# Shared PSUM slots, 4 KB loads and strided transposes in a fused recurrence and highway layer

**Chip and metric.** One core of one Trainium2 chip. The time is device microseconds (us) of one execution; every time quoted is a median over runs, every ratio a comparison on the same chip in the same rounds.

## The reference

The input is 4 sequences of 6,336 tokens with 256 channels (25,344 tokens, 26 MB in fp32). A gated recurrence runs over each sequence, and a highway layer follows:

```python
sig = 1 / (1 + exp(-f_logit))
f = lower_bound + (1 - lower_bound) * sig
for t in range(S):
    h = f[:, t] * h + (1 - f[:, t]) * x[:, t];  y[:, t] = h
H = maximum(y @ w_h, 0);  T = 1 / (1 + exp(-(y @ w_t + b_t)))
out = T * H + (1 - T) * y
```

## The kernel before

The work goes in units of 1,024 tokens (24, and one last of 768). Tokens are loaded with tokens on the partitions, but this program's scans take channels there (128x1024 in their records), so TensorE transposes in and back. One unit takes these steps; each has a letter, and the string PLAN gives the order in which they are issued, engine by engine.

- L, X: load `f_logit` and `x`. U: ScalarE makes u = sigmoid(-f_logit). P: GpSimd makes bv = u*x, two tokens at a time, interleaved so that a pair of bf16 values is one 4-byte word.
- A, B: TensorE transposes u and the pairs of bv into PSUM, the memory in which this program puts TensorE's results (`uT`, `bT`). F: ScalarE turns uT into the decay f. S: VectorE scans y = f*y + b.
- Z, G: products of y with w_t and w_h (`zp`, `gp`). T: ScalarE's sigmoid t. D: VectorE's d = max(-y, gp). E and H: e = d*t, columns shared between VectorE and GpSimd.
- O: y and e transposed back and added in PSUM (`op`), four tokens per partition a group. C and V: copies of op on ScalarE (and VectorE, for the last pieces). R: store.

In code (cuts marked; each PSUM product has a tile of its own name, hence one buffer):

```python
    BUFS = dict(lt=5, xt=5, o=8, u=4, bv=2, f=6, t=2, d=2, e=2, y=7)
    pools = {k: ctx.enter_context(tc.tile_pool(name=k + "pool", bufs=n)) for k, n in BUFS.items()}
    singles = ctx.enter_context(tc.tile_pool(name="singles", bufs=1))
    ps1 = ctx.enter_context(tc.tile_pool(name="ps1", bufs=1, space=bass.MemoryType.PSUM))

    def pairs(t):
        return t.rearrange("p (k j) d -> p k (j d)", j=2)

    def tokens(src, u, j0, j1, j):
        np_, _, b, per, a = units[u]
        if per == NB:
            return src[b, a + j0 * np_:a + j1 * np_, :].rearrange("(k p j) d -> p k (j d)", p=np_, j=j)
        return src[b + j0 // per:b + j1 // per, a:a + per * np_, :].rearrange("b (p j) d -> p b (j d)", j=per)

    def load(i, name, src):
        u, j0, j1 = fronts[i]
        np_ = units[u][0]
        t = fs[i][name] = new(name, [NB, D], FP32)
        pin(nc.sync.dma_start(pairs(t[:np_, :j1 - j0]), tokens(src, u, j0, j1, 2)))

    def gpsimd_mul(out_, a, b):
        ins = pin(nc.gpsimd.tensor_mul(out_, a, b))
        # ... cut: orders it behind the parts of e that VectorE was given before it (the list `port`) ...

    def product(i, k):
        np_, _ = shape(fronts[i])
        if k == 0:
            fs[i]["bv"] = new("bv", [NB // 2, D, 2], BF16)
        gpsimd_mul(inner(fs[i]["bv"][:np_, k:k + 1])[:, 0], fs[i]["u"][:np_, 2 * k:2 * k + 2],
                   fs[i]["xt"][:np_, 2 * k:2 * k + 2])

    def psum(piece, m, s, key, dtype):
        t = ps1.tile([P, NB * P], dtype, tag=key, name=key)
        for c, h in enumerate(halves(piece)[m]):
            s[key, h] = t[:, c * 512:c * 512 + width(piece)]
            yield s[key, h], h

    def decay_act(i, h):
        np_, N = shape(fronts[i])[0], width(fronts[i])
        f = fs[i]["f", h] = new("f", [NB * P], FP16)
        pin(nc.scalar.activation(f[:, :N].rearrange("p (k q j) -> p k q j", q=np_, j=2),
                                 fs[i]["uT", h].rearrange("p (k j q) -> p k q j", q=np_, j=2), AF.Identity,
                                 scale=ncc[:, h:h + 1], bias=1.0))

    def b_pe(i, m):
        np_, nb = shape(fronts[i])
        for bT, h in psum(fronts[i], m, fs[i], "bT", BF16):
            for k in range(nb // 2):
                pin(nc.tensor.transpose(bT[:, 2 * k * np_:2 * (k + 1) * np_].bitcast(FP32),
                                        fs[i]["bv"][:np_, k, h * P:(h + 1) * P].rearrange("p d j -> p (d j)").bitcast(FP32),
                                        ident_f[:np_, :np_]))

    # ... scan: h = f*h + b along the columns, on VectorE; ffn_pe: products with w_t and w_h; t_act, d_dve: ScalarE and VectorE ...

    SHARE = 448          # columns of e that GpSimd takes, of 1024

    def e_dve(j):
        port.append(pin(nc.vector.tensor_mul(*e_cols(j, 0, width(backs[j]) - shared(j)))))

    def e_pool(j):
        gpsimd_mul(*e_cols(j, width(backs[j]) - shared(j), width(backs[j])))

    def o_pe(j, q):
        op = bs[j]["op", q] = ps1.tile([P, QB, D], FP32, tag="op", name="op")
        (np_, nb), y = shape(backs[j]), y_of(j)
        j0, j1 = q * QB, min((q + 1) * QB, nb)
        g = min(j1 - j0, units[backs[j][0]][3])
        for k in range(j0, j1):
            b, i = divmod(k - j0, g)
            cols = slice((j0 + b * g) * np_ + i, (j0 + (b + 1) * g) * np_, g)
            for h in range(NH):
                o = op[:np_, k - j0, h * P:(h + 1) * P]
                pin(nc.tensor.matmul(o, y[:, h, cols], diag[:, h], start=True, stop=False))
                pin(nc.tensor.matmul(o, bs[j]["e"][:, h, cols], ident_b, start=False, stop=True))

    def o_copy(j, q, engine):
        np_ = shape(backs[j])[0]
        if ("o", q) not in bs[j]:
            bs[j]["o", q] = new("o", [QB, D], FP32)
        g, a = copied(j, q)
        part = slice(0, a) if engine is nc.scalar else slice(a, g)
        copy = nc.scalar.copy if engine is nc.scalar else nc.vector.tensor_copy
        pin(copy(bs[j]["o", q][:np_, part], bs[j]["op", q][:np_, part]))

    # ... kinds: one letter for each step ...
    PLAN = (
        # ... seven lines cut ...
        "OGFCTAOESDPHPPUCBZGOSDFTCBAZGORRRXRRRRXPHPUFTCSDEBAGZOSDFFTCABZGOFTCPPHRRRSSDEZGOBTFCRDGOZHSDDESCROT"
        "TCEVRGZOTTCDDVROEVCROCVR"
    )
    for k in PLAN:
        kinds[k][0](*next(todo[k]))
```

Of the kernel before, what the change touches and what calls it, by code (L numbers as in the profile page):

```python
# [19 lines left out]
def kernel(  # L20
# [43 lines left out]

    HELPED = 3



    first = ctx.enter_context(tc.tile_pool(name="first", bufs=1))
# [14 lines left out]
    def pin(ins):  # L84
        return tc.keep_in_program_order(ins)

    def pairs(t):

        return t.rearrange("p (k j) d -> p k (j d)", j=2)

    def inner(t):

        return t.rearrange("p k d j -> p k j d")
# [1 line left out]
# [6 lines that stand above are left out]

    def load(i, name, src):
        u, j0, j1 = fronts[i]
        np_ = units[u][0]
        t = fs[i][name] = new(name, [NB, D], FP32)
        pin(nc.sync.dma_start(pairs(t[:np_, :j1 - j0]), tokens(src, u, j0, j1, 2)))

    def shape(piece):

# [43 lines left out]
    def gpsimd_mul(out_, a, b):  # L153

        ins = pin(nc.gpsimd.tensor_mul(out_, a, b))  # L155
        while port:
            tc.add_manual_dep(ins.ins, port.pop().ins.name, mybir.DependencyInfo(
                mybir.DependencyClass.Sync, mybir.DependencyReason.DATA), reason="shared port")

    def product(i, k):  # L160
        np_, _ = shape(fronts[i])
        if k == 0:
            fs[i]["bv"] = new("bv", [NB // 2, D, 2], BF16)
        gpsimd_mul(inner(fs[i]["bv"][:np_, k:k + 1])[:, 0], fs[i]["u"][:np_, 2 * k:2 * k + 2],
                   fs[i]["xt"][:np_, 2 * k:2 * k + 2])

    def width(piece):
        np_, nb = shape(piece)
# [3 lines left out]

        return ((0,), (1,)) if width(piece) > 512 else ((0, 1),)

    def psum(piece, m, s, key, dtype):

        t = ps1.tile([P, NB * P], dtype, tag=key, name=key)
        for c, h in enumerate(halves(piece)[m]):
            s[key, h] = t[:, c * 512:c * 512 + width(piece)]
            yield s[key, h], h  # L180

    def decay_pe(i, m):
        np_, nb = shape(fronts[i])
        for uT, h in psum(fronts[i], m, fs[i], "uT", FP16):
            for j in range(nb):
                pin(nc.tensor.transpose(uT[:, j * np_:(j + 1) * np_], fs[i]["u"][:np_, j, h * P:(h + 1) * P],  # L186
                                        ident_h[:np_, :np_]))

    def decay_act(i, h):

        np_, N = shape(fronts[i])[0], width(fronts[i])
        f = fs[i]["f", h] = new("f", [NB * P], FP16)
        pin(nc.scalar.activation(f[:, :N].rearrange("p (k q j) -> p k q j", q=np_, j=2),  # L193
                                 fs[i]["uT", h].rearrange("p (k j q) -> p k q j", q=np_, j=2), AF.Identity,
                                 scale=ncc[:, h:h + 1], bias=1.0))

    def b_pe(i, m):
        np_, nb = shape(fronts[i])
        for bT, h in psum(fronts[i], m, fs[i], "bT", BF16):

            for k in range(nb // 2):
                pin(nc.tensor.transpose(bT[:, 2 * k * np_:2 * (k + 1) * np_].bitcast(FP32),  # L202
                                        fs[i]["bv"][:np_, k, h * P:(h + 1) * P].rearrange("p d j -> p (d j)").bitcast(FP32),
                                        ident_f[:np_, :np_]))

# [17 lines left out]
        u, j0, j1 = backs[j]  # L223
        return ys[u][:, :, j0 * units[u][0]:j1 * units[u][0]]

    def ffn_pe(j, m, key, k):
        N = width(backs[j])
        for p, h in psum(backs[j], m, bs[j], key, FP32):
            for ki in range(NH):
                for a in range(0, N, 512):  # L230
                    e = min(a + 512, N)
                    pin(nc.tensor.matmul(p[:, a:e], w_sb[:, k, ki, h * P:(h + 1) * P], y_of(j)[:, ki, a:e],  # L232
                                         start=ki == 0, stop=ki == NH - 1))
# [9 lines left out]
        pin(nc.vector.scalar_tensor_tensor(bs[j]["d"][:, m, :width(backs[j])], y_of(j)[:, m], ncc[:, m:m + 1],  # L243
                                           bs[j]["gp", m], op0=ALU.mult, op1=ALU.max))

    SHARE = 448

    def shared(j):

# [5 lines left out]
        return (bs[j][key][:, :, a:e] for key in "edt")  # L255

    def e_dve(j):
        port.append(pin(nc.vector.tensor_mul(*e_cols(j, 0, width(backs[j]) - shared(j)))))  # L258

    def e_pool(j):  # L260
        gpsimd_mul(*e_cols(j, width(backs[j]) - shared(j), width(backs[j])))

    QB = NB // 2

    def o_pe(j, q):

        op = bs[j]["op", q] = ps1.tile([P, QB, D], FP32, tag="op", name="op")
        (np_, nb), y = shape(backs[j]), y_of(j)
        j0, j1 = q * QB, min((q + 1) * QB, nb)
        g = min(j1 - j0, units[backs[j][0]][3])  # L270
        for k in range(j0, j1):
            b, i = divmod(k - j0, g)
            cols = slice((j0 + b * g) * np_ + i, (j0 + (b + 1) * g) * np_, g)
            for h in range(NH):
                o = op[:np_, k - j0, h * P:(h + 1) * P]
                pin(nc.tensor.matmul(o, y[:, h, cols], diag[:, h], start=True, stop=False))  # L276
                pin(nc.tensor.matmul(o, bs[j]["e"][:, h, cols], ident_b, start=False, stop=True))  # L277

    def copied(j, q):

        g = min(QB, shape(backs[j])[1] - q * QB)
        return g, g // 2 if j >= len(backs) - HELPED else g

    def o_copy(j, q, engine):
        np_ = shape(backs[j])[0]
        if ("o", q) not in bs[j]:
            bs[j]["o", q] = new("o", [QB, D], FP32)
        g, a = copied(j, q)
        part = slice(0, a) if engine is nc.scalar else slice(a, g)
        copy = nc.scalar.copy if engine is nc.scalar else nc.vector.tensor_copy  # L290
        pin(copy(bs[j]["o", q][:np_, part], bs[j]["op", q][:np_, part]))  # L291

    def store(j, q):
        u, j0, _ = backs[j]
        a, (g, _) = j0 + q * QB, copied(j, q)
        per = min(g, units[u][3])
        pin(nc.sync.dma_start(tokens(out_bsd, u, a, a + g, per),
                              bs[j]["o", q][:units[u][0], :g].rearrange("p (k j) d -> p k (j d)", j=per)))

    def each(pieces, count):  # L300
        return [(i, k) for i, piece in enumerate(pieces) for k in range(count(piece))]

    def groups(piece):
        return -(-shape(piece)[1] // QB)


    kinds = {
# [1 line left out]
        "X": (lambda i, _: load(i, "xt", x), each(fronts, lambda p: 1)),  # L309
        "Q": (lambda i, k: load_weights(k), [(0, 0), (0, 1)]),  # L310
        "U": (lambda i, _: gate(i), each(fronts, lambda p: 1)),
        "P": (product, each(fronts, lambda p: shape(p)[1] // 2)),
        "A": (decay_pe, each(fronts, lambda p: len(halves(p)))),
        "F": (decay_act, each(fronts, lambda p: NH)),
        "B": (b_pe, each(fronts, lambda p: len(halves(p)))),
        "S": (scan, each(fronts, lambda p: NH)),
        "W": (lambda i, h: weights(h), [(0, 0), (0, 1)]),
        "Z": (lambda j, m: ffn_pe(j, m, "zp", 1), each(backs, lambda p: len(halves(p)))),
        "T": (t_act, each(backs, lambda p: NH)),
        "G": (lambda j, m: ffn_pe(j, m, "gp", 0), each(backs, lambda p: len(halves(p)))),  # L320
        "D": (d_dve, each(backs, lambda p: NH)),
        "E": (lambda j, _: e_dve(j), each(backs, lambda p: 1)),
        "H": (lambda j, _: e_pool(j), [(j, 0) for j in range(len(backs)) if shared(j)]),
        "O": (o_pe, each(backs, groups)),
        "C": (lambda j, q: o_copy(j, q, nc.scalar), each(backs, groups)),
        "V": (lambda j, q: o_copy(j, q, nc.vector), [p for p in each(backs, groups) if p[0] >= len(backs) - HELPED]),
        "R": (store, each(backs, groups)),
    }

    PLAN = (  # L330
        "XLLXLXQQLXUUAPFFBAPSSUFFBASSWLLXLXPFFUPBAPFFUUPWSSLLXXLXPPGABZPPFFTDSSGABZUFFTDSSEAGBZFUFUTHPPPPPPDS"
        "SOGABZCFTDSSAOGHPPPPFABZDSUFCTGBZALLXLXXLLRUTUFDSBGEESDOZBAGCTUFSDPPPPHZOBASTCFGZOBAPPPPHTCFDSZGOABD"
        "ESTUCFGZOABTFCDZAGOHPPPPFTCSDEEAGBOZXXRRLRRRRLLXFUCTDSAGBOZDSPHPPPFCTAOBZGESDFCOBATUFPPPPHPPZGATFCSD"
        "BZGAOTFCUSDPPHBZGAOXRRXXLRXLRRRTFCSDEBGAZOFTCESDABZGOPPPPPPHFTUCSDABGZOSEDPPHFTCABZGOFTUCSDRRXLLXRRR"
        "XBZGAOSDTFCBAGOZPHPPPPSDEFUTCBAGZOSDFTCABZGOPPHPPSDEFTCXLLRRRRBGAOZESDUFCTBOAGZSPHPPPPPPUFTCBADSGZOB"
        "FTCDESAGOZBHPPPPUCFTDSOGAZBCTFDSOGZBAHPCTUFDEESGZOABXRRRXRLLXLLRRDSTFCPPPPPHZGAOBTFCDSZGOBAUTCDSPPPH"
        "ZGODEFTCUBZAGOFTCESDABZGOFTCUSDPPHPPHPPPABZGOSDRXRRLRRRLXTCFBZOAGSEDTCFBZAGOTUCFSDBZGOAPPPPPHTCSDEZB"
        "OGFCTAOESDPHPPUCBZGOSDFTCBAZGORRRXRRRRXPHPUFTCSDEBAGZOSDFFTCABZGOFTCPPHRRRSSDEZGOBTFCRDGOZHSDDESCROT"
        "TCEVRGZOTTCDDVROEVCROCVR"
    )  # L340
    assert all(PLAN.count(k) == len(places) for k, (_, places) in kinds.items())
    todo = {k: iter(places) for k, (_, places) in kinds.items()}
    for k in PLAN:
        kinds[k][0](*next(todo[k]))
# [1 line left out]
_INS = ['x', 'f_logit', 'lower_bound', 'moe_w_h', 'moe_w_t', 'moe_b_t']  # L346
_OUTS = [((25344, 256), 'float32')]
# [25 lines left out]
```

## Time and profile before

| | before |
|---|---|
| time | 219.93 us (3 runs, 219.38 to 220.0) |
| span of the profiled run | 219.6 us |
| VectorE / ScalarE / TensorE / GpSimd busy | 90 / 89 / 86 / 73% |
| DMA packets in the main queue | 34,176, taking 92.1% of 16 engines |

The span is what the profiler sees of one execution, about 2 us under its time. The engine lines, slices, windows, head and tail are shown in the prediction below.

### The profile page before, as it was taken

Reading aid. Unit: us, or ns where it says so; the run is one execution under the profiler, and the core shown is the slowest. Engines: PE = TensorE matmul, PEld = TensorE weight load, DVE = VectorE, ACT = ScalarE, POOL = GpSimd, SP = SyncE. Lnnn points to the kernel's source line nnn. Section 1 sums busy time; section 2 is a strip of 40 time slices with the busy share of each in tenths; the row PEclk is TensorE's granted clock in tenths of the full one; section 3 lists DMA queues with packets and bytes.
Section 4 is the critical chain, followed back from the end, with each engine's and each line's share of the span. In section 5 each row is a group of like instructions: output and inputs, shape, how many; then the busy total and the mean of one; then the engine's idle time right before and its main releaser. Section 6 shows DMA issues by size and latency. Waiting matters only on the chain.

```text
span 219.6 us, 4569 instructions
## 1 busy us (share of the span) xinstructions
PE 188.4 (86%) x1772; PEld 132.9 (61%) x1800; DVE 197.2 (90%) x154; ACT 195.4 (89%) x194; POOL 161.1 (73%) x136
## 2 busy tenths in 40 slices
PE   0578787799999999999998999999999969998840
PEld 0435554466776766776766677566767656766640
DVE  1488978999999999999999999999999997999931
ACT  3679999999999999999999999999999958987621
POOL 4758579699769697889986979599687769663200
PEclk9999999999999999999999999999999997999975
DMA  5999999999999999999999999999999992644553
GB/s 146 401 408 408 411 403 408 409 404 409 405 416 415 403 414 404 411 417 409 409 410 407 402 418 416 409 408 406 416 413 413 349 357 112 215 169 168 212 213 103
DMA packets 34741, 78.68 MB, mean 358 GB/s; under 512 B 2336, under 2 KB 2848, under 8 KB 34720
## 3 DMA queue, kind: packets, MB, share of 16 engines
q1 hardware_dynamic: 34176, 78.39, 92.1%
q8 instruction: 14, 0.23, 0.4%
q10 hardware_dynamic: 544, 0.00, 0.1%
q14 instruction: 7, 0.06, 0.1%
HBM read 52.43 MB, written 25.95 MB: 357 GB/s over the span
## 4 chain that ended last, share of the span: by engine, by line
PE 29%; DVE 25%; DMA 15%; ACT 14%; issue 9%; POOL 4%; SPq 1%; DVEq 0%; POOLq 0%; ACTq 0%
DVE y L217 13%; PE gp L232 9%; DMA xt<-in_x_dram 9%; DVE d L243 8%; PE zp L232 6%; DMA lt<-in_f_logit_dram 5%; ACT t L238 5%; ACT f L193 4%; ACT o L291 4%; PE bT L202 4%; PE op L276 4%; PE op L277 3%; PE uT L186 3%; POOL bv L155 3%; DVE e L258 2%
## 5 line engine op out<-in xcount | busy, mean ns | idle before, releaser
L155 POOL TENSOR_TENSOR bv<-u,xt 128x512 bf16<-128x512 f16 (+1 forms) x100 | 114.3, 1173 | 30.8 <-DVE e L258 8.7
L217 DVE TENSOR_TENSOR_SCAN y<-f,y,bT 128x1024 bf16<-128x1024 f16 (+3 forms) x56 | 106.7, 1919 | 2.1 <-PE bT L202 2.0
L243 DVE SCALAR_TENSOR_TENSOR d<-y,ncc,gp 128x1024 bf16<-128x1024 bf16 (+1 forms) x52 | 62.7, 1209 | 3.0 <-PE gp L232 2.9
L193 ACT ACTIVATE f<-uT,ncc 128x1024 f16<-128x1024 f16 (+3 forms) x60 | 59.7, 1007 | 2.3 <-PE uT L186 2.3
L291 ACT COPY o<-op 128x1024 f32<-128x1024 f32 (+2 forms) x50 | 51.1, 1021 | 10.8 <-PE op L277 8.1
L238 ACT ACTIVATE t<-zp,bt 128x1024 bf16<-128x1024 f32 (+1 forms) x52 | 58.0, 1120 | 1.9 <-PE zp L232 1.0
L232 PEld LDWEIGHTS <-w_sb 128*128 128x128 f16 x400 | 38.2, 99 | 35.3 <-issue 4.4
L276 PE MATMUL op<-diag,y 128*128 128x128 f16 (+1 forms) x400 | 51.6, 222 | 3.5 <-ACT o L291 1.8
L155 POOL TENSOR_TENSOR e<-d,t 128x896 bf16<-128x896 bf16 x24 | 45.9, 1911 | 11.8 <-DVE e L258 5.0
L232 PE MATMUL gp<-y,w_sb 128*128 128x512 bf16 (+1 forms) x189 | 51.8, 387 | 2.9 <-DVE d L243 1.5
L277 PE MATMUL op<-ident_b,e 128*128 128x128 bf16 (+1 forms) x400 | 51.6, 222 | 2.5 <-POOL e L155 2.2
L149 ACT ACTIVATE u<-lt 128x2048 f16<-128x2048 f32 (+3 forms) x30 | 49.6, 1657 | 3.3 <-DMA lt<-in_f_logit_dram 3.1
L277 PEld LDWEIGHTS <-e 128*128 128x128 bf16 (+1 forms) x400 | 45.5, 116 | 10.6 <-issue 3.3
L232 PE MATMUL zp<-y,w_sb 128*128 128x512 bf16 (+1 forms) x183 | 49.5, 377 | 0.9
L276 PEld LDWEIGHTS <-y 128*128 128x128 bf16 (+1 forms) x400 | 45.7, 116 | 3.9
L186 PE MATMUL uT<-ident_h,u 128*128 128x128 f16 (+1 forms) x400 | 32.5, 227 | 8.6 <-ACT u L149 6.8
L202 PE MATMUL bT<-ident_f,bv 128*128 128x128 f32 (+1 forms) x200 | 32.4, 284 | 7.5 <-DVE y L217 5.9
L186 PEld LDWEIGHTS <-u 128*128 128x128 f16 (+1 forms) x400 | 27.5, 102 | 16.6 <-ACT u L149 8.2
L202 PEld LDWEIGHTS bT<-ident_f,bv 128*128 128x128 f32 (+1 forms) x200 | 22.0, 144 | 14.9 <-issue 5.5
L258 DVE TENSOR_TENSOR e<-d,t 128x1152 bf16<-128x1152 bf16 (+1 forms) x26 | 20.7, 817 | 0.5 <-ACT t L238 0.5
L217 DVE TENSOR_TENSOR_SCAN y<-f,bT 128x512 bf16<-128x512 f16 (+2 forms) x8 | 10.5, 1341 | 3.6 <-PE bT L202 3.6
L291 DVE COPY o<-op 128x512 f32<-128x512 f32 (+1 forms) x4 | 2.8, 690 | 4.8 <-DMA out_dram<-o 3.2
(19 smaller groups left out, 7.5 us busy)
## 6 DMA issues: line engine op xcount, KB each, us to landing
out_dram<-o SPq DMA_DIRECT2D x48, 512.0 KB, 11.4
lt<-in_f_logit_dram SPq DMA_DIRECT2D x21, 1024.0 KB, 13.9
xt<-in_x_dram SPq DMA_DIRECT2D x21, 1024.0 KB, 13.9
lt<-in_f_logit_dram SPq DMA_DIRECT2D x5, 512.0 KB, 8.0
xt<-in_x_dram SPq DMA_DIRECT2D x5, 512.0 KB, 9.1
lt<-in_f_logit_dram SPq DMA_DIRECT2D x2, 384.0 KB, 11.4
xt<-in_x_dram SPq DMA_DIRECT2D x2, 384.0 KB, 5.4
out_dram<-o SPq DMA_DIRECT2D x2, 384.0 KB, 3.0
```

The costliest lines, as they stand in the source:

```text
L149: pin(nc.scalar.activation(u[:np_, :nb], fs[i]["lt"][:np_, :nb], AF.Sigmoid, scale=-1.0))
L155: ins = pin(nc.gpsimd.tensor_mul(out_, a, b))
L186: pin(nc.tensor.transpose(uT[:, j * np_:(j + 1) * np_], fs[i]["u"][:np_, j, h * P:(h + 1) * P], ident_h[:np_, :np_]))
L193: pin(nc.scalar.activation(f[:, :N].rearrange("p (k q j) -> p k q j", q=np_, j=2), fs[i]["uT", h].rearrange("p (k j q) -> p k q j", q=np_, ...
L202: pin(nc.tensor.transpose(bT[:, 2 * k * np_:2 * (k + 1) * np_].bitcast(FP32), fs[i]["bv"][:np_, k, h * P:(h + 1) * P].rearrange("p d j -> ...
L217: pin(nc.vector.tensor_tensor_scan(y, fs[i]["f", h][:, c:c + w], fs[i]["bT", h][:, c:c + w], 0.0 if prev is None else prev, op0=ALU.mult, ...
L232: pin(nc.tensor.matmul(p[:, a:e], w_sb[:, k, ki, h * P:(h + 1) * P], y_of(j)[:, ki, a:e], start=ki == 0, stop=ki == NH - 1))
L238: pin(nc.scalar.activation(bs[j]["t"][:, m, :width(backs[j])], bs[j]["zp", m], AF.Sigmoid, bias=bt[:, m:m + 1]))
L243: pin(nc.vector.scalar_tensor_tensor(bs[j]["d"][:, m, :width(backs[j])], y_of(j)[:, m], ncc[:, m:m + 1], bs[j]["gp", m], op0=ALU.mult, op1 ...
L276: pin(nc.tensor.matmul(o, y[:, h, cols], diag[:, h], start=True, stop=False))
L277: pin(nc.tensor.matmul(o, bs[j]["e"][:, h, cols], ident_b, start=False, stop=True))
L291: pin(copy(bs[j]["o", q][:np_, part], bs[j]["op", q][:np_, part]))
```

## The change

Its intent: longer runs in the loads; a second PSUM buffer for whichever product needs one; and with it a regular order of issue.

```diff
-        pin(nc.sync.dma_start(pairs(t[:np_, :j1 - j0]), tokens(src, u, j0, j1, 2)))
+        pin(nc.sync.dma_start(t[...].rearrange("p (k j) d -> p k (j d)", j=j), tokens(src, u, j0, j1, j)))
+    def run(piece):                       # tokens per partition: 4 tokens of 1 KB
+        return min(4, j1 - j0, units[u][3])
-        t = ps1.tile([P, NB * P], dtype, tag=key, name=key)
+        tag = ("one" if dtype in (FP16, BF16) else "two") + slot    # slot: digit behind the letter in PLAN
+        return ps1.tile([P, *shape], dtype, tag=tag, name=key)
     # decay_act: the rearrange takes j = run(...) in place of 2
     # b_pe:
-                pin(nc.tensor.transpose(bT[:, 2 * k * np_:2 * (k + 1) * np_].bitcast(FP32), ...
+            t = bT.bitcast(FP32).rearrange("p (k q j) -> p k j q", q=np_, j=r)      # r = 2
+                pin(nc.tensor.transpose(t[:, k // r, k % r], ...       # every second 4-byte word
-    SHARE = 448
+    SHARE = 512
     # PLAN: a new order; A, B, Z, G, O carry a slot: two slots of 2 KB for A and B, three of 4 KB for Z, G, O
-    ... ZGOBTFCRDGOZHSDDESCROTTCEVRGZOTTCDDVROEVCROCVR
+    ... FFTDSZ2G1G0A0HTFSDDEZ2B1Z1O0FTTTSEHO2CSG1CRZ0RG2DTDTEDO1O0CVDVO1CERRCVO2RCVR
```

The slots take the same 16 KB of each partition's PSUM as the five tiles before. The diff also holds two switches that are left off (copies of half a group at the very end, products on VectorE).

## The prediction

> **What bounds the kernel now.** I read the busy shares first, then the slices, then busy time in windows of 20 us, then the head and the tail instruction by instruction.
>
> ```profile
> PE 188.4 (86%) x1772; PEld 132.9 (61%) x1800; DVE 197.2 (90%) x154; ACT 195.4 (89%) x194; POOL 161.1 (73%) x136
> DMA  5999999999999999999999999999999992644553
> GB/s 146 401 408 408 411 403 408 409 404 409 405 416 415 403 414 404 411 417 409 409 410 407 402 418 416 409 408 406 416 413 413 349 357 112 215 169 168 212 213 103
> q1 hardware_dynamic: 34176, 78.39, 92.1%
> ```
>
> No single engine stands out: VectorE 90%, ScalarE 89%, TensorE 86%, and the DMA engines full at about 410 GB/s until some 175 us. The windows say where the idle time is:
>
> ```profile
> 0.00:20.00 20.00, 10.54 (x63) 6.70 (x64) 10.95 (x17) 13.32 (x20) 11.87 (x21) 1.00 0.93 334
> 20.00:40.00 20.00, 15.36 (x126) 9.81 (x128) 17.62 (x15) 19.79 (x19) 16.11 (x14) 1.00 1.05 407
> 100.00:120.00 20.00, 19.02 (x194) 13.90 (x196) 19.92 (x14) 20.00 (x19) 17.34 (x15) 1.00 1.04 410
> 180.00:200.00 20.00, 19.15 (x179) 13.66 (x183) 18.77 (x16) 16.71 (x19) 13.78 (x11) 0.91 0.45 169
> 200.00:220.00 20.00, 10.84 (x120) 8.48 (x118) 10.39 (x17) 7.57 (x12) 1.89 (x1) 0.79 0.46 171
> ```
>
> Columns after the length: PE, PEld, DVE, ACT, POOL busy, then clock, DMA share, GB/s. In the middle DVE and ACT are both busy all of the 20 us. Of DVE's 22.8 us of idle time (220 - 197.2), 11.4 lie before 40 us and 10.8 after 180 us. So the middle is bound by two engines at once, and the change can only win much at the two ends.
>
> The pace of the middle: between the 8th and the 36th copy of results (63.68 and 168.75 us), 14 units of 1024 tokens go by, 105.07 / 14 = 7.5 us each. Starts of back-to-back instructions give ACT 1.80 (u) + 2 x (1.0 f + 1.0 t + 0.9 copy) = 7.6 us a unit and DVE 2 x (2.26 scan + 1.18 d) + 0.75 e = 7.6. From rows and the pitch inside groups PE has some 7.0: 16 products of 512 columns at 0.217, 32 output products and 16 transposes of u at 0.056, 8 of b at 0.113. DMA needs 3.15 MB / 410 GB/s = 7.7. ACT waits only 3.1 us for f_logit in the whole run, so the full DMA queue is not yet what is waited for in the middle: loads live on the lead of five buffers. In the head it is:
>
> ```profile
> 30.06 4.54 POOL L155 TENSOR_TENSOR bv<-u,xt 128x512 bf16<-128x512 f16 x4 [1.48 <-DMA xt<-in_x_dram]
> 42.76 3.43 POOL L155 TENSOR_TENSOR bv<-u,xt 128x512 bf16<-128x512 f16 x3 [1.83 <-DMA xt<-in_x_dram]
> ```
>
> All five waits of the products for x (6.8 us in sum) are before 43 us. In the tail the single PSUM tile for outputs is what is passed round:
>
> ```profile
> 205.09 0.22 PE L276 MATMUL op<-diag,y 128*128 128x128 f16 x1 [0.45 <-ACT o L291]
> 210.02 0.22 PE L276 MATMUL op<-diag,y 128*96 128x128 f16 x1 [1.40 <-DVE o L291]
> 212.46 0.26 PE L276 MATMUL op<-diag,y 128*96 128x128 f16 x1 [1.39 <-ACT o L291]
> 211.11 0.69 DVE L291 COPY o<-op 96x512 f32<-96x512 f32 x1 [0.68 <-PE op L277]
> 214.97 0.69 DVE L291 COPY o<-op 96x512 f32<-96x512 f32 x1 [3.18 <-DMA out_dram<-o]
> ```
>
> The last scan ends at 206.1 us; from there to the end of the span is 13.5 us, in which DVE works only about 5 us.
>
> [...] the packet records have a median of 84 ns for 2 KB and 159 ns for 4 KB, so two short ones cost 9 ns more than a long one, 5% of 168. [...] a slot is refilled only after its reader is done: these are the waits on copies above. [...] the products on POOL wait 8.7 us in 6 places for the VectorE e, though the program itself orders some of these.
>
> **The change part by part.**
>
> 1. SHARE 448 to 512: VectorE's e has 1024 elements in place of 1152. From 839 ns, in proportion, some 750: 24 x 0.07 to 0.09 = about 1.9 us less on DVE. POOL's e grows from 1911 to about 1911 x 1024/896 = 2184 ns, 24 x 0.27 = 6.5 us more, to some 168 of 220 us: it still has room. As ACT keeps its 7.6 us a unit, I count 1 to 1.5 us.
>
> 2. Loads with 4 KB runs: 12,900 packets of 4 KB in place of 25,700 of 2 KB. Saved 12,864 x 9 ns / 16 engines = 7 us of DMA time. The queue's share should fall from 92% towards 89% of the same span, and full rate rise from 410 to about 425 GB/s, or 7.4 us a unit. In the middle this is hidden: nothing waits there. In the head, which loads fill, it is 5% of some 35 us, 1.7 us at most; the new order, which brings x sooner after its f_logit, helps the same waits. I count 1 to 2 us.
>
> 3. The order on ACT for decay (four tokens gathered in place of two) reads PSUM with the same step between neighbours; 42 instructions of 1176 ns stay. No change.
>
> 4. Transposes of b into every second word: at most 192 of them, now at a pitch of 0.113 us, twice that of a 16-bit transpose (0.056). If the fp32 stream is the limit, the wider write is hidden; if each costs twice, PE gets 8 x 0.113 = 0.9 us a unit, 7.9 in all, above the 7.5 of the others. I expect the first and put a quarter on some cost: 0 to 8 us, counted as 1.
>
> 5. PSUM slots shared: two of 2 KB for the transposes, three of 4 KB for zp, gp and op, as many bytes as before. Every product can now have a second buffer while another needs none. The plan changes from an irregular order to a repeated one (on ACT, f t t u f c c; on DVE, d e s d s). It takes away the tail's waits: outputs of neighbouring groups go to slots 1 and 0, so that the PE fills one (about 1 us) while the other is copied. DVE's instructions after its last scan add up to 4 d or e-like steps and four copies, about 5.5 us; with one output product (1 us) and the same last store and end (4 us) the 13.5 us become some 10. I count 3 us. In the middle DVE's gaps are about 2 us in all, so there is little to win and something to lose: a slot shared by three products couples them[...]. I count 0.5 us lost.
>
> Sum: -1.3 - 1.5 + 1 - 3 + 0.5 = -4.3 us, and some 1 us more for the gaps of DVE and ACT between 160 and 200 us (ACT waits there 2.83 us for one output product). 219.9 - 5.3 = about 214.7 us.
>
> **Rivals.** (a) PE becomes the bound through the strided transposes. For: 96% busy in the middle[...]. Against: PE's pitch sums to 7.0 of 7.5 us, and fp32 transposes already run at half the pace. It would make 222 to 228 us. (b) ACT alone holds the time: its work is untouched, its 195 us start at 5 us, and if the middle stays at 7.5 us and the tail's waits are merely moved to the last d, e and stores, the result is 217 to 219. For: ACT full in nearly every middle window. Against: its idle time of 10.7 us between 180 and 215 us is made of waits for output products, which the slots loosen. (c) The DMA was the hidden bound: needs 7.7 us a unit against 7.5. Then 4 KB runs speed the whole load phase by up to 7 us and, with the tail, the time goes to 209 to 211. Against: no waits for loads after 43 us.
>
> **Range and chances.** The centre of the sum is 214.7. (b) is the nearest rival and keeps the upper end near 219.8; (c) or a tail better than I think gives 210. The 2% line is at 215.5, close to the centre: faster by over 2% 0.56, within 2% 0.38, slower by over 2% (rival (a)) 0.06.
>
> **What would show it.** Right: packets of 4 KB alone in the loads and a full rate of 420 GB/s or more; e on DVE near 750 ns, on POOL near 2.2 us; pitch of the b transposes still near 0.11 us; the distance from the last scan to the end near 10 us; DVE idle before 40 us down to 9 or 10. Wrong: b transposes at twice the pitch and DVE waiting for bT in the middle; unit time in the middle clearly off 7.5 us in either direction; waits of PE for slot readers of several us in sum between 60 and 160 us.

The sum keeps all its terms: -4.3 us, with 1 us for the gaps -5.3, and 219.9 - 5.3 = about 214.7 us.

## The result and the profile after

The changed kernel took **216.03 us** (4 runs, 215.95 to 216.13) against 219.66 us (4 runs, 219.16 to 220.0) in the same rounds: ratio **0.9837**, 95% interval 0.9814 to 0.986. That is 1.6% faster: inside the predicted range, 1.3 us above its centre, and on the "within 2%" side, which had 0.38 against 0.56 for faster. (A ratio is the mean time of one kernel's fast runs over that of the other's in the same rounds, so not quite the quotient of the medians.)

The page of the profile after: busy times, rate in 40 slices, main queue.

```profile
PE 185.9 (87%) x1776; PEld 131.2 (61%) x1800; DVE 195.5 (91%) x154; ACT 194.4 (91%) x194; POOL 168.0 (78%) x136
GB/s 134 418 410 421 422 416 394 312 413 418 416 420 422 417 420 415 420 420 418 421 416 420 421 416 421 419 412 422 416 377 257 390 419 364 250 100 299 95 250 197
q1 hardware_dynamic: 22144, 78.39, 92.6%
```

Fewer packets and a rate near 420 GB/s, but a slice of 312 at about 40 us that the kernel before did not have. Windows of the kernel after (start:end, length, then busy TensorE, weight loads, VectorE, ScalarE, GpSimd, clock, DMA share, GB/s):

```profile
0.00:20.00 20.00, 9.54 (x52) 6.68 (x54) 10.53 (x16) 12.01 (x19) 12.64 (x21) 1.00 0.91 341
20.00:40.00 20.00, 17.48 (x166) 12.03 (x166) 19.52 (x17) 19.23 (x19) 17.77 (x15) 1.00 1.01 402
180.00:200.00 20.00, 18.99 (x196) 13.59 (x196) 19.97 (x18) 18.43 (x23) 14.74 (x11) 1.00 0.50 200
200.00:220.00 20.00, 7.27 (x96) 5.86 (x93) 7.62 (x14) 5.44 (x9) 2.13 (x1) 0.84 0.39 145
```

VectorE now idles almost nothing from 20 us to 200 us. To see where time went, I use VectorE's scans as milestones, since they come in the same sequence in both orders: the start of the 8th and of the 36th scan over 1,024 columns (14 units apart), the end of the last scan, the end of the span. "before_again" is another profile of the kernel before (mean clock 0.996), "oldplan" is an experiment below: the code of the change, but the order of before with one slot per product.

| us | before_again | oldplan | after |
|---|---|---|---|
| 8th scan starts | 60.41 | 59.85 | 60.74 |
| 8th to 36th (14 units) | 106.46 | 106.44 | 107.03 |
| 36th to the end of the last scan | 37.93 | 36.06 | 33.97 |
| last scan to end of span | 12.72 | 13.51 | 12.23 |
| span | 217.5 | 215.9 | 214.0 |
| VectorE idle in these four stretches | 11.4, 0.6, 0.5, 8.0 | 11.3, 0.8, 0.5, 8.8 | 10.8, 1.2, 0.0, 6.4 |

The spans differ by 3.5 us, the medians by 3.6. None of it comes from the middle. In the stretch between 167 and 205 us there are two steps, of 1.9 and 2.1 us. The first, from before_again to oldplan, is a gain: VectorE runs the same instructions there. The second, from oldplan to after, is mostly work that was moved: the new order has done one e more before the 8th scan, and leaves two d more for behind the last scan, so VectorE is busy 1.6 us less in between (33.9 against 35.5 us); the rest is its idle time of 0.5 us, which is gone. So this stretch has to be read together with the tail: there the new order does more work in less time, and VectorE idles 6.4 us in place of 8.0.

**The clock at the end.** One difference in the table is not the order's or the loads'. In every profile the granted clock falls near the end (to 0.50 in windows of half a us, from 212.0 us on in before and from 210.0 us on in after), but not at the same place (before_again, oldplan, after):

```profile
PEclk9999999999999999999999999999999999999998
PEclk9999999999999999999999999999999999999985
PEclk9999999999999999999999999999999999999996
```

With the order of before, the last scan is followed by 13.5 us where the clock falls 5.4 to 6.2 us after it (before, b_4kb, oldplan), and by 12.7 us where it falls 8.3 or 10.8 us after it (b_share512, before_again). The 0.8 us stand in ScalarE's wait for the last output product, in before_again and in oldplan:

```profile
212.25 0.58 ACT L291 COPY o<-op 96x512 f32<-96x512 f32 x1 [1.14 <-PE op L277]
210.59 0.58 ACT L303 COPY o<-op 96x512 f32<-96x512 f32 x1 [1.95 <-PE op L297]
```

In after it falls 8.2 us behind the last scan, so its 12.23 us are to be compared with 12.7. The timed runs show the same: the two of oldplan with a mean clock of 0.99 or more took 216.7 us, the four near 0.98 took 217.6.

### The profile page after: what moved, and what is told of

The parts are those of the page before. It is cut to its first block, busy times and chain, and to the rows that moved or that the text cites. A ratio compares the mean times of both kernels' runs of the same rounds, so it can differ in the third digit from the quotient of the medians.

```text
span 214.0 us, 4567 instructions
## 1 busy us (share of the span) xinstructions
PE 185.9 (87%) x1776; PEld 131.2 (61%) x1800; DVE 195.5 (91%) x154; ACT 194.4 (91%) x194; POOL 168.0 (78%) x136
## 3 DMA queue, kind: packets, MB, share of 16 engines
q1 hardware_dynamic: 22144, 78.39, 92.6%
## 4 chain that ended last, share of the span: by engine, by line
ACT 36%; DMA 32%; PE 14%; issue 7%; DVE 6%; POOL 2%; SPq 1%; DVEq 0%; ACTq 0%; POOLq 0%
DMA out_dram<-o 16%; DMA lt<-in_f_logit_dram 13%; ACT f L205 11%; ACT t L251 10%; ACT o L303 9%; ACT u L154 6%; PE gp L245 3%; DVE y L230 3%; PE zp L245 3%; DMA xt<-in_x_dram 3%; PE uT L198 2%; PE bT L215 2%; PE op L297 2%; PE op L296 2%; DVE d L256 1%
## 5 line engine op out<-in xcount | busy, mean ns | idle before, releaser
L160 POOL TENSOR_TENSOR bv<-u,xt 128x512 bf16<-128x512 f16 (+1 forms) x100 | 115.7, 1179 | 19.8 <-DVE e L166 7.2
L205 ACT ACTIVATE f<-uT,ncc 128x1024 f16<-128x1024 f16 (+3 forms) x60 | 64.0, 1081 | 3.7 <-PE uT L198 3.7
L160 POOL TENSOR_TENSOR e<-d,t 128x1024 bf16<-128x1024 bf16 x24 | 51.1, 2128 | 14.6 <-DVE e L166 11.8
L251 ACT ACTIVATE t<-zp,bt 128x1024 bf16<-128x1024 f32 (+1 forms) x52 | 56.9, 1192 | 1.6 <-POOL e L160 0.9
L154 ACT ACTIVATE u<-lt 128x2048 f16<-128x2048 f32 (+3 forms) x30 | 52.1, 1736 | 5.2 <-DMA lt<-in_f_logit_dram 4.9
L303 ACT COPY o<-op 128x1024 f32<-128x1024 f32 (+2 forms) x50 | 49.8, 1114 | 2.5 <-DVE o L303 1.9
L296 PE MATMUL op<-diag,y 128*128 128x128 f16 (+1 forms) x400 | 49.2, 219 | 1.6 <-ACT t L251 0.7
L245 PE MATMUL gp<-y,w_sb 128*128 128x512 bf16 (+1 forms) x186 | 49.0, 377 | 1.5 <-ACT t L251 0.8
L297 PE MATMUL op<-ident_b,e 128*128 128x128 bf16 (+1 forms) x400 | 49.1, 220 | 1.0 <-DVE e L166 0.5
L166 DVE TENSOR_TENSOR e<-d,t 128x1024 bf16<-128x1024 bf16 (+1 forms) x26 | 18.1, 700 | 1.8 <-ACT t L251 0.5
(19 smaller groups left out, 10.8 us busy)
## 6 DMA issues: line engine op xcount, KB each, us to landing
out_dram<-o SPq DMA_DIRECT2D x48, 512.0 KB, 12.7
```

The costliest lines, as they stand in the source:

```text
L154: pin(nc.scalar.activation(u[:np_, :nb], fs[i]["lt"][:np_, :nb], AF.Sigmoid, scale=-1.0))
L245: pin(nc.tensor.matmul(p[:, a:e], w_sb[:, k, ki, h * P:(h + 1) * P], y_of(j)[:, ki, a:e], start=ki == 0, stop=ki == NH - 1))
L251: pin(nc.scalar.activation(bs[j]["t"][:, m, :width(backs[j])], bs[j]["zp", m], AF.Sigmoid, bias=bt[:, m:m + 1]))
L303: pin(copy(bs[j]["o", q][:np_, a:e], bs[j]["op", q][:np_, a:e]))
```

## The experiments

Twelve runs in three batches of four, on chips 1, 2 and 15, each batch beside 11 runs of the kernel before (medians 219.78, 220.08 and 220.14 us). Ratios are to those of the same batch. The theories: (A) the gain is in the tail (the part behind the last scan), where the slots remove waits on `op`; (B) the loads give it, because transfers were late somewhere; (C) SHARE gives it, because VectorE is the bound; (D) ScalarE alone holds the middle.

### First batch: which part of the change does it

**b_share512**: the kernel before, one number changed.

```diff
-    SHARE = 448
+    SHARE = 512
```

> The kernel before with SHARE 512 alone. VectorE's e should fall from 839 to about 715 ns (24 of them, 3 us of DVE time), POOL's e rise from 1911 to about 2130. Theory ACT (ScalarE, 7.6 us a unit, sets the middle): at most 1 us faster, 218.7 to 219.7. Rival DVE (VectorE sets the middle): 2 to 3 us faster, 216.7 to 217.7.

Measured 219.84 us, ratio 1.0002 (0.9959 to 1.0044). SHARE alone gives nothing; (C) falls for the old order.

**b_4kb**: the loads, the decay order and the strided transposes alone.

```diff
 # the code after, with the PLAN of before, each product in a slot of its own (A0 B1 Z0 G1 O2)
-    SHARE = 512
+    SHARE = 448
```

> The kernel before with its own order and private PSUM buffers and SHARE 448, but loads in 4 KB runs and the transposes of b into every second word. Theory ACT: only the head gains, 0 to 1.5 us: 218.2 to 219.7. Rival DMA (the full DMA queue was a hidden bound): 4 us or more faster, under 216. If the strided transposes cost anything, slower than 220, with a pitch above 0.11 us.

Measured 217.07 us, ratio 0.9876 (0.9841 to 0.9911): 2.7 us, three quarters of the whole gain, with neither shared slots nor the new order: more than the 0 to 1.5 us that I expected, less than the 4 of the rival. And the strided transposes cost nothing. The group of b's transposes, first in before_again, then in b_4kb (busy us, mean ns of one):

```profile
L202 PE MATMUL bT<-ident_f,bv 128*128 128x128 f32 x192 | 31.6, 285 | 7.0 <-DVE y L217 5.5 <-POOL bv L155 1.2
```

```profile
L215 PE MATMUL bT<-ident_f,bv 128*128 128x128 f32 x192 | 31.3, 285 | 6.6 <-DVE y L230 5.7 <-POOL bv L160 0.6
```

285 ns in both, and the median from one start to the next is 0.109 us in both (and in the trace after): rival (a) of the prediction is out.

**oldplan**: the same with SHARE 512.

```diff
 # the code after, with the PLAN of before, each product in a slot of its own (A0 B1 Z0 G1 O2); SHARE = 512 stays
```

> Everything of the change except the shared slots and the new order: 4 KB loads, strided transposes and SHARE 512 in the old order with private buffers. If order and slots carry the gain (theory): 218 to 219, so at most a third of the 3.6 us. If loads and SHARE carry it (rival): 216 to 217.

Measured 217.56 us, ratio 0.9874 (0.9841 to 0.9908): as b_4kb, and better than the 218 to 219 us that I expected. VectorE's e, in b_4kb and in oldplan:

```profile
L166 DVE TENSOR_TENSOR e<-d,t 128x1152 bf16<-128x1152 bf16 x24 | 17.6, 759 | 0.5 <-ACT t L251 0.5
```

```profile
L166 DVE TENSOR_TENSOR e<-d,t 128x1024 bf16<-128x1024 bf16 x24 | 16.4, 709 | 0.5 <-ACT t L251 0.5
```

The smaller share saves 50 ns an e, 1.2 us of VectorE's time in all, and the kernel is no faster. So why did the mean of 839 ns in the kernel before promise more? Most e took about 0.75 us there too. A single pair took over 3 us, and that pair is where the gain of the 4 KB loads is.

**a_share448**: the kernel after with the old share.

```diff
-    SHARE = 512
+    SHARE = 448
```

> The changed kernel with SHARE back at 448, so 24 x 0.126 = 3 us more work on DVE. Theory ACT: the middle keeps 7.64 us a unit and DVE's 7.4 rises to 7.5, still below: 0 to 0.7 us slower, 216.0 to 216.7. Rival DVE: 2.5 to 3 us slower, 218.5 to 219.

Measured 216.49 us, ratio 0.9838 (0.9803 to 0.9873), against 0.9837 for the whole change in its own rounds. In its trace the 14 units of the middle take 107.34 us against 107.03 after: in the new order the share shows in the middle of the trace, but by 0.3 us, and not in the ratios.

**Where the loads gain.** The same stretch, 176 to 182 us, in before_again (GpSimd, VectorE and ScalarE in order of time; start, length, operation, idle time before and what the profile takes as its end):

```profile
176.77 1.17 POOL L155 TENSOR_TENSOR bv<-u,xt 128x512 bf16<-128x512 f16 x1 [2.10 <-PE op L277]
177.89 2.43 POOL L155 TENSOR_TENSOR e<-d,t 128x896 bf16<-128x896 bf16 x1
177.83 3.11 DVE L258 TENSOR_TENSOR e<-d,t 128x1152 bf16<-128x1152 bf16 x2
181.33 1.01 ACT L291 COPY o<-op 128x1024 f32<-128x1024 f32 x1 [2.45 <-PE op L277]
```

and in b_4kb:

```profile
169.50 5.68 POOL L160 TENSOR_TENSOR bv<-u,xt 128x512 bf16<-128x512 f16 x5 [1.14 <-ACT o L303]
175.13 1.90 POOL L160 TENSOR_TENSOR e<-d,t 128x896 bf16<-128x896 bf16 x1
177.21 1.43 DVE L166 TENSOR_TENSOR e<-d,t 128x1152 bf16<-128x1152 bf16 x2
179.09 1.01 ACT L303 COPY o<-op 128x1024 f32<-128x1024 f32 x1 [0.83 <-PE op L297]
```

In before_again GpSimd's product waits 2.10 us, put down to TensorE, which does not even write its input. The chain of what ended last names another cause:

```profile
163.70 1.75 POOL e L155
165.45 11.16 DMA xt<-in_x_dram
176.77 1.17 POOL bv L155
177.94 2.39 POOL e L155
```

It is the load of x of the last full unit, on its way for 11.16 us. It is late, so GpSimd's e is late, and falls on the very moment at which VectorE starts two e of its own. GpSimd's record grows from 1.90 to 2.43 us, VectorE's two from 1.43 to 3.11 us. Of these two it is the second alone: it starts at 178.50 us, and ends at 180.94, 0.6 us after GpSimd's e (180.32). So it looks like a wait for GpSimd's, and not like a slower pace. Then the output product comes late, and ScalarE sits 2.45 us. In b_4kb the load is issued 1.7 us earlier (163.78 us) and lands after 9.15 us, at 172.93 in place of 176.61 us; the fifth product follows the others without a gap, e is over before VectorE starts its own, and the next copy on ScalarE starts at 179.09 in place of 181.33 us. b_share512 has the accident in a worse form: there the two e on VectorE took 3.83 us, although each has fewer columns, which is why its mean was still 830 ns. From the 36th scan to the scan behind the two e it is 13.99 us in before_again and 12.29 in b_4kb: these 1.7 us are the whole difference of the stretch. So the loss of the kernel before lay at one spot, counted as *busy* time of VectorE. That the late load is its cause is read from the chain and from the times of landing; no run moved this load alone. Whether in other runs of before the accident always has this size is not known; all three of its profiles (two of before, one with SHARE 512) show it.

### Second batch: loads and slots inside the new order

**a_2kb**: the kernel after with pairs of tokens, as before.

```diff
-        return min(4, j1 - j0, units[u][3])
+        return min(2, j1 - j0, units[u][3])
```

> The changed kernel with two neighbouring tokens per partition again: 2 KB runs and contiguous transposes, all else as changed. Theory ACT: middle unchanged at 7.64 us a unit as long as loads keep ahead; head loses 0 to 1.5 us: 216 to 217.5. Rival DMA: at 410 GB/s a unit needs 7.7 us, above the 7.64, with ACT waiting for f_logit in the middle: 218 to 220. If strided transposes cost PE time that matters, this is faster than 216.

Measured 218.64 us, ratio 0.9906 (0.9861 to 0.9951): slower than after by 2.6 us in the medians and in the spans (216.6 against 214.0), by 1.5 us in the ratios. But here the loss is in the head: its 8th scan starts at 63.42 us against 60.74, and from then on it stays 2.7 us behind (36th scan 170.45 against 167.77, last scan's end 204.45 against 201.74). So 4 KB runs are worth about as much in both orders, at different places. (One of its six runs took 217.02 us, so the loss is not in every run.)

**a_tail1**: the new order, but the last output products all in one slot, one behind the other's copies.

```diff
-    ... TDTEDO1O0CVDVO1CERRCVO2RCVR
+    ... TDTEDO1CVO1DCVO1ERRCVO1RCVR
```

> The changed kernel with its last four output products in one slot, each filled only after the copies of the one before (the order of the last letters adapted to that). Theory (the shared slots shorten the tail): 1 to 3 us slower, 217 to 219. Rival (the tail is shorter only because the DVE work before it ended earlier): 0 to 0.5 us slower.

Measured 219.9 us, ratio 0.9961 (0.9919 to 1.0003). Last scan to end: 16.30 us against 12.23. Part of this is the clock, which fell 6.5 us after the last scan; its two runs with a mean clock of 0.989 and 0.990 took 218.28 and 218.85 us. So at a like clock the loss is some 2.2 to 2.8 us: without a second slot the new order would give most of its gain back.

**a_actlight**: less work on ScalarE, with a wrong result on purpose (relative error 0.93): f and t become plain copies.

```diff
-        pin(nc.scalar.activation(f..., uT..., AF.Identity, scale=ncc[:, h:h + 1], bias=1.0))
+        pin(nc.scalar.copy(f..., uT...))
-        pin(nc.scalar.activation(t..., zp..., AF.Sigmoid, bias=bt[:, m:m + 1]))
+        pin(nc.scalar.copy(t..., zp...))
```

> Wrong results on purpose: the activations f and t of the changed kernel become plain copies of the same shapes, which need no per-partition scale or bias. Pitch of f and t should fall from 1.0 to about 0.9 us, 0.4 us of ScalarE time a unit, 10 us in all. Theory ACT: the unit in the middle goes from 7.64 to the 7.4 of DVE or the 7.5 of the DMA, 3 to 5 us faster, 211 to 213. Rival DVE or DMA as the bound: less than 1 us faster.

Measured 215.51 us, ratio 0.9777 (0.974 to 0.9814): 0.5 us below the kernel after by medians, 1.3 us by ratios. From 60 to 160 us, the kernel after and then a_actlight:

```profile
60.00:160.00 100.00, 95.13 (x934) 67.45 (x945) 98.86 (x66) 100.00 (x93) 87.64 (x66) 1.00 1.03 417
```

```profile
60.00:160.00 100.00, 95.92 (x936) 68.25 (x947) 98.95 (x67) 97.32 (x94) 87.45 (x66) 1.00 1.03 419
```

ScalarE now has idle time, VectorE is as full as it was, and the pace hardly moves: 14 units in 106.40 us against 107.03. The 3 to 5 us that I expected did not come. Theory (D) falls for the new order: with ScalarE relieved, VectorE holds the kernel at 7.60 us a unit.

**before_again**: no edit, one look, for a profile at full clock.

> The kernel before once more, for a second profile. Its first profiled run took 221.41 us, 1.7 above the median, with a granted clock of 0.79 to 0.91 in the last 40 us. Expected: a run of about 219.7 with a span near 217.8; the missing 1.7 us lies in the tail if the clock there is higher, and then the tail's gain in the change is 2.3 us rather than 4.0.

Measured 219.31 us (one run), span 217.5 us; used above.

**The middle, worked out.** Pitches (start to start) from the traces, ScalarE in both orders: u 1.80, f and t 1.00, copy 0.90, so a unit takes 1.80 + 2 x (1.00 + 1.00 + 0.90) = 7.60 us. VectorE in the order of before: 2 x (2.26 scan + 1.17 d) + 0.67 e = 7.53 us, and 7.46 with SHARE 512 (e at 0.60). The measured unit is 7.604 in before_again and 7.603 in oldplan (106.46 and 106.44 over 14): ScalarE's sum, and blind to SHARE. That the match is so close is luck in part: in these 14 units of before_again ScalarE starts 97 instructions in place of 98 (104.5 us of pitches) and loses 1.5 us in pitches longer than usual. And no run relieved ScalarE in the order of before, so that it sets the pace there is argued from these figures. In the new order VectorE has one thing more. Middle of the trace after:

```profile
101.34 1.25 DVE L256 SCALAR_TENSOR_TENSOR d<-y,ncc,gp 128x1024 bf16<-128x1024 bf16 x1
102.69 0.69 DVE L166 TENSOR_TENSOR e<-d,t 128x1024 bf16<-128x1024 bf16 x1
103.30 2.34 DVE L230 TENSOR_TENSOR_SCAN y<-f,y,bT 128x1024 bf16<-128x1024 f16 x1
105.56 1.26 DVE L256 SCALAR_TENSOR_TENSOR d<-y,ncc,gp 128x1024 bf16<-128x1024 bf16 x1
106.73 2.34 DVE L230 TENSOR_TENSOR_SCAN y<-f,y,bT 128x1024 bf16<-128x1024 f16 x1
112.61 1.28 DVE L256 SCALAR_TENSOR_TENSOR d<-y,ncc,gp 128x1024 bf16<-128x1024 bf16 x1
113.81 0.68 DVE L166 TENSOR_TENSOR e<-d,t 128x1024 bf16<-128x1024 bf16 x1
```

A scan starts 1.17 us after d (105.56 to 106.73), but e 1.35 us after d (101.34 to 102.69). This e reads what the d just before it wrote. The last two lines are a place where the d belongs to a later unit: 1.20 us. In the trace after, all 12 pairs of the first kind in the regular part have 1.35 to 1.37 us, and all 5 of the second have 1.17 to 1.20. In the order of before, no e follows the d of its own unit at once, and all its pairs have 1.17 to 1.20. So the regular order costs 0.19 us for each such unit. In the 14 units of the middle, where 4 of 14 e escape, VectorE's sum becomes 2 x 2.256 (scan) + 1.17 + 1.31 (d) + 0.61 (e) = 7.60 us, equal to ScalarE's; together they run at 7.645. With SHARE 448 (e at 0.67) it is 7.66, and a_share448 ran at 7.667. a_actlight, with ScalarE out of the way, ran at 7.600. The four measured paces lie within 0.05 us of the larger sum. In this trace the dependence took 0.19 us, and an instruction in between took it away.

### Third batch: what the slots are worth, and a better version

**old_tail**: oldplan, with shared slots in the last letters only, and these letters in an order that suits them.

```diff
-    ... TTCEVRG1Z0O2TTCDDVRO2EVCRO2CVR
+    ... TTCEVRG1Z0TTO0DDECVRO2CVRO1CVR
```

> The old order with 4 KB loads, strided transposes and SHARE 512, and the shared slots used in the last letters only: the last four output products go to slots 2, 0, 2, 1, so that none waits for the copies of the one before, and VectorE's last e is done before its last copies. If the wait for one output buffer is what the slots remove (theory), the stretch from the last scan to the end falls from 13.5 us by 2.5 to 4: 213.5 to 215.0 us, faster than the changed kernel with its new order. Rival (the tail is bound by the copies and the last store whatever the slots): 216.5 to 217.5, as the old order without them.

Measured 215.86 us, ratio 0.9811 (0.9772 to 0.985), against 217.56 us and 0.9874 for oldplan (in another batch). Last scan to end: 11.63 us against 13.51, of which 0.8 us is the clock (it fell 7.8 us after the last scan, in oldplan 6.2). The last copies on VectorE, in oldplan and in old_tail:

```profile
207.34 0.69 DVE L303 COPY o<-op 96x512 f32<-96x512 f32 x1 [0.68 <-PE op L297]
211.21 0.69 DVE L303 COPY o<-op 96x512 f32<-96x512 f32 x1 [3.18 <-DMA out_dram<-o]
```

```profile
207.43 0.69 DVE L303 COPY o<-op 96x512 f32<-96x512 f32 x1 [0.20 <-ACT o L303]
208.32 0.69 DVE L303 COPY o<-op 96x512 f32<-96x512 f32 x1 [0.20 <-ACT o L303]
```

The wait of 3.18 us is gone. Theory (A) holds for the tail: 1.4 us by ratios and 1.9 by spans, but 0.8 us against the two runs of oldplan at a like clock (216.7), and 1.1 us between this tail and that of before_again. The 2.5 to 4 us that I expected did not come, for a reason that the traces show: from the last scan to the end of the last copy it is 8.75 us in before_again and 6.73 here, but from there to the end 3.97 and 4.90, as the last stores, issued 0.9 us apart, take longer to land (3.9 us for the last, against 3.0). And the order of before, with three slots for three products at the end, equals the whole change: the rest of the new order adds nothing on balance. (The two were timed in different batches.)

**old_tail_q2**: the same, and the very last outputs in groups of two tokens, each copied by one engine.

```diff
-    LASTQ = 4
+    LASTQ = 2
-    ... TTO0DDECVRO2CVRO1CVR
+    ... TTO0DDECVRO2CVRO1O0CVRR
```

> As old_tail, and the last piece is given out in two halves, one copied by ScalarE and one by VectorE, each stored by itself. The last store is 192 KB in place of 384 and starts after one copy: 0.2 to 0.8 us faster than old_tail. Rival: two stores in a row cost as much as the bytes they save, within 0.2 us of old_tail.

Measured 215.63 us, ratio 0.9799 (0.976 to 0.9837): 0.2 us, within the noise.

**a_head**: the kernel after, with the first store issued behind the next loads.

```diff
-    ... DB1A0Z1G0G2ESRXLRLLXRXL
+    ... DB1A0Z1G0G2ESXLRRLLXRXL
```

> The changed kernel with one swap in the order of DMA issues: the first store goes behind the two loads that follow it, since loads were held from 20 to 33.5 us behind a store that waited for its data. Theory (the new order starves ScalarE of f_logit between 40 and 50 us for that reason): the DMA rate from 35 to 45 us returns from 345 to 420 GB/s, ScalarE's waits for f_logit fall by 1 us or more, 0.5 to 1.5 us faster: 214.5 to 215.5. Rival (these loads waited for buffers anyway): within 0.3 us of 216.0.

In the kernel after, the queue of loads and stores issues nothing from 20.3 to 33.5 us: the first store stands in front and waits for its copy (13.1 us, put down to ScalarE's copy), and the next loads go out behind it, from 33.95 us on. That is the slice of 312 GB/s. The window of 35 to 45 us, in after and in a_head:

```profile
35.00:45.00 10.00, 9.71 (x103) 7.00 (x102) 9.90 (x9) 9.20 (x10) 8.62 (x8) 1.00 0.96 347
```

```profile
35.00:45.00 10.00, 9.76 (x93) 6.60 (x92) 9.90 (x8) 9.86 (x11) 8.64 (x8) 1.00 1.03 418
```

The hole is filled, but the kernel took 215.85 us, ratio 0.9802 (0.9765 to 0.9839): not clearly different from after, and its 8th scan starts at 60.78 against 60.74. The hole cost nothing that can be shown.

**a_best**: a_head with LASTQ = 2.

```diff
-    LASTQ = 4
+    LASTQ = 2
-    ... DB1A0Z1G0G2ESRXLRLLXRXL ... VDVO1CERRCVO2RCVR
+    ... DB1A0Z1G0G2ESXLRRLLXRXL ... VDVO1CERRCVO2O0RCVRR
```

> a_head with the last piece given out in two halves as in old_tail_q2: 0.2 to 0.8 us faster than a_head, 214.0 to 215.2. Rival: as a_head.

Measured **214.97 us** (214.39 to 215.44), ratio 0.9768 (0.9731 to 0.9804): 2.3% faster than before, though the interval touches the 2% line, so whether it is more than 2% is unclear (against the five runs of before with a clock of 0.989 or more, median 219.41 us, it is 2.0%), and 1.1 us below after by medians. It beats both kernels. Of the 1.4 us by which its span is shorter (212.6 us), 0.5 us lie behind the last scan (11.78 against 12.23 us) and 0.7 before the 8th (60.06 against 60.74). Since a_head alone shows nothing of the latter, I cannot say that its cause is understood.

**Left open.** In the tail, ScalarE's and VectorE's copies of one tile run one after the other (VectorE's wait before its copy is put down to ScalarE's copy, 0.67 us and 0.40 us at the end of the trace after), at some 0.6 us each time; I did not find out why. Why LASTQ = 2 gave 0.2 us in one order and perhaps 0.9 in the other is open too. An order in which e runs a unit later has not been tried; with ScalarE at 7.60 us the sums give it at most 0.05 us a unit. And why the clock falls earlier in some runs than in others, no run here shows.

## Why the prediction was right or wrong

The measured 216.03 us lies in its range, 1.3 us above its centre, but that owes something to luck: several terms were wrong, and their errors cancelled in part. Step by step:

**What bounds the kernel.** Two engines at once in the middle: right, and a_actlight shows it from the other side. The pace of 7.5 us was misread: I took it from copies of results, which drift against the scans; the scans give 7.60, which is ScalarE's sum. With that in hand, it could be seen that VectorE had 0.07 us to spare in each unit and that step 1 would buy nothing.

**Step 1, SHARE (-1 to -1.5 us): wrong.** Measured 1.0002 alone, and 0.3 us of the middle inside the new order. It failed twice. The 839 ns was a mean over 22 good e and a pair that ran beside GpSimd's late e (3.27 us for the two in the profile of before): the true e was 759 and went to 709 ns. And the 1.2 us that VectorE really saved lay beside ScalarE's longer sum. GpSimd's e came out at 2,128 ns (foreseen: 2,184), without harm.

**Step 2, loads (-1 to -2 us): the size too small, the place wrong.** The rate came as foreseen (410 to about 420 GB/s), and the head gave 0.6 us. Packets fell by 12,032 and not 12,864: 1,664 of 2 KB are left in the loads, so the sign "packets of 4 KB alone" failed. The queue's packet time fell by some 4 us (from 93.0% of 217.5 to 92.6% of 214.0), not by 7. What failed is the sentence "In the middle this is hidden: nothing waits there." The wait was in the trace that I had: GpSimd's product started at 176.7 us after 2.30 us of idle time, put down to a ScalarE sigmoid. I looked only at waits that named a transfer. The measured term is 2.7 us by medians; before the last scan the milestones show 0.6 + 1.9 = 2.5 us. Rival (c), the hidden DMA bound, was partly true: not for the pace, but for the one late load.

**Step 3, decay order (0): right** as far as can be told: no run changed it alone, and ScalarE's pitch of f is 1.00 us before and after.

**Step 4, strided transposes (+1): it was 0**, the branch that I called likelier; 285 ns in both.

**Step 5, slots and order.** Middle +0.5: measured +0.59 (107.03 against 106.44), now with a cause, the e that waits for its own d. Head: I expected the new order to help. It came 0.9 us later to the 8th scan (60.74 against 59.85), though with one e more done by then. Gaps between 160 and 200 us, -1: VectorE's idle time from the 36th scan to the last went from 0.5 to 0.0 us, so -0.5; the other 1.6 of the 2.1 us in the table are work put elsewhere. Tail, 13.5 to 10 us: measured 12.23. **The tail is the term that was mis-sized**, for three reasons. Its 13.5 us came from a profile in which the clock fell early; at a like clock it is 12.7. The new order moves work there: I took 5.5 us of VectorE work, four d or e and four copies; there are four d, two e and four copies, some 6.3 us of record, and the copies of two engines still pass one tile on to each other, so that the last copy ends 7.7 us after the last scan, not 6. And the last store with the end takes 4.5 us, not 4. In VectorE's idle time the tail gained 1.6 us of the 3. The slots themselves do what was claimed: without them a_tail1 loses 2.2 to 2.8 us at a like clock, and with them old_tail gains 0.8 to 1.1.

In sum, by spans and at a like clock: loads -2.4 (head -0.6, the one spot with SHARE -1.9), new order and slots +0.9 + 0.6 - 2.1 - 0.5 = -1.1; together -3.5 us of the -5.3 foreseen. The two timed runs of oldplan at a like clock agree: 216.7 to 216.03 us.

## What to carry to other kernels

Sum the start-to-start pitches of each engine over one repeat, and compare them closely: relief for the second-longest sum bought nothing here (1.2 us less of VectorE's time from b_4kb to oldplan, ratios 0.9876 and 0.9874). A mean over a group can hide one accident, and a stretched instruction counts as busy (here two e in 3.11 us, and in 1.43 where they were not stretched), so look at the longest of a group and follow the chain back through it; the releaser named beside a wait may be wrong (here TensorE, beside a wait of 2.10 us), and a late load is a suspect where the DMA queue is full (here 11.16 us on its way, at some 410 GB/s). When two orders are compared by milestones, count the instructions between them, since work that was moved looks like a gain; and compare ends of runs only where the clock falls at a like place (here it was worth 0.8 us). And in an order for VectorE, put another instruction between one that writes and one that reads the result (here 0.19 us each time).

## What the runs showed of the hardware

- Writing fp32 transposes into every second 4-byte word cost nothing: 285 ns a transpose in both forms, and 0.109 us from start to start.
- Packets of 2 KB took 84 ns, of 4 KB 159 ns (medians in the trace of before). The loads ran at 410 against some 420 GB/s, and in time it was 2.7 us of 220 in the old order, 1.5 to 2.6 in the new.
- In before_again a VectorE e beside GpSimd's took 2.44 us, where 0.75 us is usual, and ended 0.6 us after GpSimd's. If that was a wait, as it looks, it stands in the record as busy time.
- An e that reads the d right before it starts 0.19 us later than one that does not (1.36 against 1.17 us, 12 and 5 cases in the trace after).
- ScalarE's records changed in length while its pitch stayed: f reads 1,176 ns before and 1,283 after, with the same pitch of 1.00 us. So take pitches, not records, for its sums.
